# Seven half-size products for a down projection, with attention regrouped, in a PE-bound fused kernel

## The chip, the cores and the metric

The kernel runs on one core of a Trainium2 chip. The metric is device time in microseconds (us). TensorE (PE) does the matmuls, VectorE (DVE) and ScalarE (ACT) read its results out of PSUM, GpSimd (POOL) works in SBUF, and the queues of SP, ACT and POOL start transfers. A profile is one execution recorded by the hardware; its span is a little shorter than the timed runs of the same kernel (301.4 against 302.2 us before).

## The reference, cut to what matters

```python
k_p = k.reshape(B, H, Sp, 8, D).mean(axis=3)      # v_p likewise; B = H = 8, S = 576, Sp = 72, D = 64
attn = softmax(q @ k_p.T / sqrt(D));  x = attn @ v_p          # -> 4608 tokens x 512
h = x @ w_in                                       # 512 -> 2048, "up"
g = h * cos(h)
out = g @ w_out                                    # 2048 -> 512, "down"
```

## The kernel before: the parts that the change and the argument touch

Tokens go in nine tiles of 512. Tile t runs an up stage and a down stage; between the down matmuls of tiles 1 to 6 stands the attention of batch t+1, cut into four units (256 tokens x 4 heads), and of a rest segment (the last 64 tokens of batch t, all heads). PSUM has eight banks: three pairs, used in turn by the up stage and by attention, and two single banks for the down sums.

```python
def up_g(t, fp, between=()):                       # 8 per tile
    cos = ...; nc.scalar.activation(out=cos, in_=h, func=ACTF.Sin, bias=half_pi[:, :1])
    nc.vector.tensor_mul(out=g_sb[:, 2 * fp:2 * fp + 2, :], in0=h, in1=cos)

def down_mm(o, ms, fc):                            # 64 per tile, 512 columns each
    nc.tensor.matmul(o, lhsT=g_sb[:, fc, ms * 128:(ms + 1) * 128], rhs=w_out_sb[fc // 4][:, fc % 4, :], ...)

def values(b, u, pair, later=None):                # values and sums of one unit in one matmul, two halves
    ...
    for hp in range(2):
        nc.scalar.activation(out=lnc[half[1 - hp]], in_=pair[half[1 - hp], hp, 0:w], func=ACTF.Ln)
    nc.scalar.activation(out=inv, in_=lnc, func=ACTF.Exp, scale=-1.0)      # 1/sum
    ...                                            # two half multiplies into xT

def pool_add(b, which):                            # POOL sums of k and v for batch b
    add(out=s, in0=x[:, :, 0:4, :], in1=x[:, :, 4:8, :], op=ADD)           # one 4.06 us instruction
    ...
# steady tile: attention spread over the 64 down matmuls
fill = [(4, scores_of((b, us[0], 2), (b, us[1], 0))), (14, V_(0, 1, later)), (16, lambda: later.pop()()),
        (19, V_(1, 2)), (35, scores_of((b, us[2], 0), (b, us[3], 1), (t, REST, 2))),
        (38, V_(2, 0)), (43, lambda: values(t, REST, banks[1])), (46, V_(3, 2))]
```

The softmax here doesn't subtract the row's maximum and nothing guards it: scores larger than these inputs give would overflow.

## Time and profile before

| | before |
|---|---|
| time, median of the runs beside the changed kernel | 302.17 us |
| steady tile (tiles 2 to 6) | 31.30 us |
| up stage / rest of the tile | 13.85 / 17.45 us |
| PE's part of the chain that ended last | 93% |
| DVE, ACT, POOL busy | 57%, 68%, 43% |

The chain that ended last is followed back from the last instruction: each piece is what released the next one. Where it consists of PE pieces alone, nothing but PE's own stream sets the time. The prediction below shows those lines.

### The profile page before, as it was taken

The numbers are of one execution on the slowest core, as the hardware profiler recorded it, in microseconds if no ns is written. First come the engines' busy times: TensorE is split into PE (matmuls) and PEld (weight loads), VectorE is DVE, ScalarE is ACT, GpSimd is POOL, SyncE is SP. The second block draws the span as 40 slices with busy tenths as digits, with TensorE's granted clock in tenths as the row PEclk, the third lists the DMA queues.
The fourth block names the chain that finished last, engine by engine and source line by source line (L and its number), as shares of the span: only waits on it lengthen the run. The fifth ranks groups of instructions, "written<-read, shape, count | busy, mean of one in ns | idle before, by whom it ended". The sixth has DMA issues, their size and how long they took to land.

```text
span 301.4 us, 4625 instructions
## 1 busy us (share of the span) xinstructions
PE 293.9 (97%) x1816; PEld 143.2 (48%) x1816; DVE 170.8 (57%) x212; ACT 205.7 (68%) x254; POOL 130.4 (43%) x93
## 2 busy tenths in 40 slices
PE   8789999999999999999999999999999999999995
PEld 3445544445544454445444544455444544444444
DVE  5448637465467446754666556654775477425712
ACT  3786798469876987688778886789668966605500
POOL 8463016984983398239913990389300000000000
PEclk9999999999999999999999999999999999999999
DMA  7999999639526961697079617791811130131023
GB/s 152 197 207 206 206 205 195 141 55 176 117 60 124 167 127 29 146 158 140 6 170 143 129 36 171 94 174 39 141 32 35 37 70 0 37 70 35 0 67 75
DMA packets 44165, 32.91 MB, mean 109 GB/s; under 512 B 22128, under 2 KB 39408, under 8 KB 44144
## 3 DMA queue, kind: packets, MB, share of 16 engines
q0 software_dynamic: 19744, 18.07, 38.3%
q1 hardware_dynamic: 24160, 14.42, 20.5%
q8 instruction: 14, 0.23, 0.3%
q10 hardware_dynamic: 240, 0.13, 0.2%
q14 instruction: 7, 0.06, 0.1%
HBM read 36.70 MB, written 9.44 MB: 153 GB/s over the span
## 4 chain that ended last, share of the span: by engine, by line
PE 93%; DMA 4%; POOL 1%; DVE 1%; issue 0%; POOLq 0%; DVEq 0%
PE bank L297 41%; PE obank L310 41%; PE bank L241 5%; DMA kv_st<-in_v_dram 4%; PE bank L211 3%; PE bank L328 1%; PE bank L165 1%; POOL q_b L84 1%; PE obank L157 0%; PE obank L280 0%; PE obank L192 0%; DVE xT L282 0%; DVE vz L167 0%; POOL kv_st L84 0%; DVE o_sb L316 0%
## 5 line engine op out<-in xcount | busy, mean ns | idle before, releaser
L310 PE MATMUL obank<-w_out_sb,g_sb 128*128 128x512 bf16 x560 | 131.4, 379 | 0.0
L297 PE MATMUL bank<-xT,w_in_sb 128*128 128x512 bf16 x576 | 126.6, 379 | 0.0
L304 ACT ACTIVATE cos<-bank,half_pi 128x1024 f32<-128x1024 f32 x72 | 79.3, 1113 | 59.5 <-PE bank L297 59.5
L307 DVE TENSOR_TENSOR g_sb<-bank,cos 128x1024 bf16<-128x1024 f32 x72 | 87.3, 1223 | 43.0 <-ACT cos L304 42.9
L297 PEld LDWEIGHTS <-w_in_sb 128*128 128x128 bf16 x576 | 56.1, 98 | 67.6 <-issue 1.6
L310 PEld LDWEIGHTS <-g_sb 128*128 128x128 bf16 x560 | 52.8, 98 | 56.5 <-issue 2.0
L252 DVE TENSOR_TENSOR xT<-bank,inv 64x512 bf16<-64x512 f32 (+1 forms) x72 | 45.3, 629 | 40.8 <-ACT inv L248 40.1
L141 POOL TENSOR_TENSOR kv_st<-kv_st 72x2048 f32<-72x2048 bf16 x12 | 48.7, 4058 | 33.9 <-DMA kv_st<-in_k_dram 33.9
L247 ACT ACTIVATE lnc<-bank 64x512 f32<-64x512 f32 (+1 forms) x72 | 39.2, 544 | 3.1 <-PE bank L241 1.7
L316 DVE COPY o_sb<-obank 128x512 f32<-128x512 f32 x35 | 23.6, 689 | 30.9 <-PE obank L310 30.5
L218 ACT ACTIVATE ex<-bank 72x1024 bf16<-72x1024 f32 (+1 forms) x40 | 35.0, 929 | 8.5 <-PE bank L211 8.4
L142 POOL TENSOR_TENSOR kv_st<-kv_st 72x1024 f32<-72x1024 f32 x12 | 28.2, 2349 | 1.0
L248 ACT ACTIVATE inv<-lnc 128x512 f32<-128x512 f32 (+1 forms) x36 | 21.0, 583 | 1.1
L241 PE MATMUL bank<-ex,vz 72*128 72x256 bf16 (+1 forms) x176 | 20.0, 243 | 0.0
L241 PEld LDWEIGHTS <-vz 72*128 72x128 bf16 x176 | 13.6, 97 | 9.6 <-DVE xT L252 0.5
L145 POOL TENSOR_TENSOR kp<-kv_st 72x512 bf16<-72x512 f32 x12 | 14.9, 1263 | 0.5
L211 PE MATMUL bank<-qT,kk 64*72 64x256 bf16 (+1 forms) x192 | 13.2, 252 | 0.0
L211 PEld LDWEIGHTS <-kk 64*72 64x72 bf16 x192 | 7.4, 109 | 9.9 <-issue 7.2
L285 ACT ACT_TABLE_LOAD x9 | 11.5, 1283 | 0.9 <-PEq L519 0.7
L499 POOL COPY gate<-kk 1x1 bf16<-1x1 bf16 x5 | 0.9, 179 | 25.7 <-DMA kk<-kp 25.7
L288 ACT ACT_TABLE_LOAD x9 | 11.5, 1283 | 0.2
L103 POOL DMA_DIRECT2D kv_st<-in_v_dram x6 | 5.0, 841 | 8.8 <-PE bank L165 8.8
(55 smaller groups left out, 93.1 us busy)
## 6 DMA issues: line engine op xcount, KB each, us to landing
out_dram<-o_sb SPq DMA_DIRECT2D x70, 128.0 KB, 2.4
kv_st<-in_v_dram POOLq DMA_DIRECT2D x8, 576.0 KB, 13.7
kv_st<-in_k_dram POOLq DMA_DIRECT2D x7, 576.0 KB, 7.6
q_b<-in_q_dram POOLq DMA_DIRECT2D x6, 576.0 KB, 9.9
w_in_sb<-in_moe_w_in_dram POOLq DMA_DIRECT2D x4, 512.0 KB, 14.5
w_out_sb<-in_moe_w_out_dram POOLq DMA_DIRECT2D x4, 512.0 KB, 18.1
q_b<-in_q_dram POOLq DMA_DIRECT2D x4, 288.0 KB, 13.0
g_sb<-in_k_dram SPq DMA_DIRECT2D x1, 576.0 KB, 3.7
```

Source lines behind the costliest of these rows:

```text
L141: add(out=s, in0=x[:, :, 0:4, :], in1=x[:, :, 4:8, :], op=ADD)
L142: add(out=s[:, :, 0:2, :], in0=s[:, :, 0:2, :], in1=s[:, :, 2:4, :], op=ADD)
L211: nc.tensor.matmul(pair[:Sp, bank, c:c + n].rearrange("p (g n) -> p g n", n=64), lhsT=kk[b % 2][half[r], h0 + i, 0:Sp], rhs=att["qT", b][h ...
L218: nc.scalar.activation(out=ex[:, 0:nh * n].rearrange("p (a n) -> p a n", a=2), in_=pair[:Sp, :, 0:nh * n // 2], func=ACTF.Exp, scale=scale ...
L241: nc.tensor.matmul(pair[:, hp, (i // 2) * n:(i // 2 + 1) * n], lhsT=vz[b % 2][:, pj, 2 * hp:2 * hp + 2, :].rearrange("p a d -> p (a d)"), ...
L247: nc.scalar.activation(out=lnc[half[1 - hp]], in_=pair[half[1 - hp], hp, 0:w], func=ACTF.Ln)
L252: nc.vector.tensor_mul(out=x_out(b, u, half[hp]), in0=cols(pair[half[hp], hp, :], u), in1=cols(inv[half[1 - hp]], u))
L297: nc.tensor.matmul(h[:, j, :], lhsT=w_in_sb[fc // 4][:, ki, (fc % 4) * 128:(fc % 4 + 1) * 128], rhs=xT[:, ki, t * TILE:(t + 1) * TILE], st ...
L304: nc.scalar.activation(out=cos, in_=h, func=ACTF.Sin, bias=half_pi[:, :1])
L307: nc.vector.tensor_mul(out=g_sb[:, 2 * fp:2 * fp + 2, :], in0=h, in1=cos)
L310: nc.tensor.matmul(o, lhsT=g_sb[:, fc, ms * 128:(ms + 1) * 128], rhs=w_out_sb[fc // 4][:, fc % 4, :], start=(fc == 0), stop=(fc == FFCH - 1))
L316: nc.vector.tensor_copy(out=o[:, 0:n], in_=ps)
```

## The change

The intent is to do less on PE. A block product of 2 x 2 blocks takes seven half-size products of sums in place of eight. Three sums of the weights (w2, w3, w4) and one difference in place are made once; four sums of g (g1 to g4) are made on DVE in each tile; the products collect in the two down banks, and copies and adds take results out between them. Since DVE gets new work, attention is regrouped so that sums and values lie on all 128 partitions: half as many logarithms and multiplies. POOL's sums are cut into pieces of 512 elements. From tile 1 on the up stage takes the two halves of its 2048 columns in turns, so that g1 and g2 can be formed while it runs.

```diff
+    def values_of(parts, later):
+        weights = (lambda b, h: ones[:Sp, :]), (lambda b, h: vz[b % 2][:, h // 2, 3 * (h % 2), :])
+        for bank in range(2):                      # sums in one bank of the pair, values in the other
+            for b, u, pair in parts: ... nc.tensor.matmul(pair[hp * 64:hp * 64 + 64, bank, ...], ...)
+        for b, u, pair in parts: ... Ln, Exp; later.append(multiply)
 ...
+        A, Bb = obanks[1], obanks[0]
+        products = [
+            (A, True, part(g_part(0, 0, 0, HF)), of(w_out_sb[0:2])),
+            (A, False, part(g_part(1, 0, 0, HF)), of(w_out_sb[2:4])),
+            (Bb, True, part(g2), of(w2)),
+            (A, True, part(g1), of(w_out_sb[0:2], 1)),
+            (Bb, False, part(g3), of(w3)),
+            (A, False, part(g4), of(w_out_sb[2:4], 1)),
+            (Bb, False, part(g_part(1, 1, 0, HF)), of(w4)),
+        ]
+        reads = [
+            lambda: nc.scalar.copy(out=p1, in_=A),
+            lambda: nc.scalar.copy(out=o1[:, :, 0:HM], in_=two(A)),
+            lambda: add(v16, Bb, p1),
+            lambda: add(q15, A, p1),
+            lambda: add(o2[:, :, HM:], two(Bb), two(q15)),
+            lambda: (add(o1[:, :, HM:], two(A), two(v16)), rows_out(t, 0, o1)),
+            lambda: (add(o2[:, :, 0:HM], two(Bb), two(p1)), rows_out(t, 1, o2)),
+        ]
 ...
+            first = [(b, us[i], banks[i]) for i in range(3)] if steady else ...
+            second = [(b, us[3], banks[0]), (t, REST, banks[1])] if steady else []
+            product(0); reads[0](); exp_tables()          # (cut and joined)
+            scores of first;  product(1); reads[1](); g3
+            product(2); reads[2](); g4a;  product(3); reads[3](); g4b
+            values_of(first, later); later.pop(0)()
+            product(4); reads[4]();  the other multiplies
+            scores of second;  product(5); reads[5]()
+            values_of(second, later), multiplies;  product(6); reads[6]()
 ...
+                if n in range(41, 59, 3):                 # tile 0: the six weight sums on DVE
+                    weights.pop(0)()
```

Products are counted from 1 in the text: "product 1" is `product(0)`.

More of the change, by code (lines that the diff above doesn't have):

```diff
@@ L13 @@
 ADD = mybir.AluOpType.add
+SUB = mybir.AluOpType.subtract
 POOL = 8
@@ L64 @@
     g_sb = wpool.tile([128, FFCH, TILE], BF16, name="g_sb")
+    HF, HT, HM = FFCH // 2, TILE // 2, d_model // 2
+    g1, g2, g3, g4 = [wpool.tile([128, HF, HT], BF16, name=f"g{i}") for i in range(1, 5)]
+    w2, w3, w4 = [[wpool.tile([128, 4, HM], BF16, name=f"w{k}{i}") for i in range(2)] for k in range(2, 5)]
     SpA = -(-Sp // 16) * 16
@@ L70 @@
     vz = [wpool.tile([Sp, KCH, 4, D], BF16, name=f"vz{i}") for i in range(2)]
+    half_sums = wpool.tile([Sp, H, POOL // 2, D], FP32, name="half_sums")
     banks = [psum.tile([128, 2, 512], FP32, name=f"bank{i}") for i in range(3)]
@@ L86, in kv_tile @@
     def kv_tile():
-        return kvst.tile([128, 2 * H * POOL * D], BF16, name="kv_st", tag="kv_st")
+        return kvst.tile([128, 2 * KCH * ROW * D], BF16, name="kv_st", tag="kv_st")
     def even_part(st, i):
@@ L100, in load_kv @@
     def load_kv(b, which, src):
-        st = kv_tile()[:Sp].rearrange("p (i h t d) -> p i h t d", i=2, h=H, t=POOL)
-        nc.gpsimd.dma_start(out=st[:, 0].rearrange("p h t d -> p h (t d)"),
+        st = kv_tile()[:Sp, 0:H * POOL * D].rearrange("p (h t d) -> p h t d", h=H, t=POOL)
+        nc.gpsimd.dma_start(out=st.rearrange("p h t d -> p h (t d)"),
                             in_=src[b].rearrange("h (p t) d -> p h (t d)", t=POOL))
@@ L136, in pool_add @@
         st = staged.pop((which, b))
-        x = st[:, 0]
-        s = st[:, 1].rearrange("p h t d -> p (h t d)").bitcast(FP32).rearrange(
-            "p (h t d) -> p h t d", h=H, t=POOL // 2)
+        x, s = st, half_sums
         add = nc.gpsimd.tensor_tensor
-        add(out=s, in0=x[:, :, 0:4, :], in1=x[:, :, 4:8, :], op=ADD)
-        add(out=s[:, :, 0:2, :], in0=s[:, :, 0:2, :], in1=s[:, :, 2:4, :], op=ADD)
+        for h in range(0, H, 2):
+            add(out=s[:, h:h + 2], in0=x[:, h:h + 2, 0:4, :], in1=x[:, h:h + 2, 4:8, :], op=ADD)
+        for h in range(0, H, 4):
+            add(out=s[:, h:h + 4, 0:2, :], in0=s[:, h:h + 4, 0:2, :], in1=s[:, h:h + 4, 2:4, :], op=ADD)
         if which == "k":
@@ L230, in inverse_tile @@
     def inverse_tile(w):
-        lnc = asb.tile([128, 512], FP32, name="lnc", tag="lnc", bufs=1)
         inv = asb.tile([128, 512], FP32, name="inv", tag="inv", bufs=3)
-        return lnc[:, 0:w], inv[:, 0:w]
+        return inv[:, 0:w]
     def values(b, u, pair, later=None):
@@ L244, in values @@
         w = nh * n // 2
-        lnc, inv = inverse_tile(w)
+        inv = inverse_tile(w)
         for hp in range(2):
-            nc.scalar.activation(out=lnc[half[1 - hp]], in_=pair[half[1 - hp], hp, 0:w], func=ACTF.Ln)
-        nc.scalar.activation(out=inv, in_=lnc, func=ACTF.Exp, scale=-1.0)
+            nc.scalar.activation(out=inv[half[1 - hp]], in_=pair[half[1 - hp], hp, 0:w], func=ACTF.Ln)
+        nc.scalar.activation(out=inv, in_=inv, func=ACTF.Exp, scale=-1.0)
         def mul():
@@ L258, in values @@
             later.append(mul)
+    def values_of(parts, later):
+        weights = (lambda b, h: ones[:Sp, :]), (lambda b, h: vz[b % 2][:, h // 2, 3 * (h % 2), :])
+        for bank in range(2):
+            for b, u, pair in parts:
+                (c0, n), (h0, nh) = u
+                ex = att["ex", b, u]
+                for i in range(nh):
+                    hp = i % 2
+                    nc.tensor.matmul(pair[hp * 64:hp * 64 + 64, bank, (i // 2) * n:(i // 2 + 1) * n],
+                                     lhsT=weights[bank](b, h0 + i), rhs=ex[:, ex_col(u, i):ex_col(u, i) + n])
+        for b, u, pair in parts:
+            att.pop(("ex", b, u))
+            w = u[1][1] * u[0][1] // 2
+            inv = inverse_tile(w)
+            nc.scalar.activation(out=inv, in_=pair[:, 0, 0:w], func=ACTF.Ln)
+            nc.scalar.activation(out=inv, in_=inv, func=ACTF.Exp, scale=-1.0)
+            later.append(lambda b=b, u=u, pair=pair, inv=inv: nc.vector.tensor_mul(
+                out=x_out(b, u, slice(0, 128)), in0=cols(pair[:, 1, :], u), in1=cols(inv, u)))
     def sums_first(b, u, cs):
@@ L268, in sums_first @@
         w = nh * n // 2
-        lnc, inv = inverse_tile(w)
-        nc.scalar.activation(out=lnc, in_=cs[:, 0:w], func=ACTF.Ln)
-        nc.scalar.activation(out=inv, in_=lnc, func=ACTF.Exp, scale=-1.0)
+        inv = inverse_tile(w)
+        nc.scalar.activation(out=inv, in_=cs[:, 0:w], func=ACTF.Ln)
+        nc.scalar.activation(out=inv, in_=inv, func=ACTF.Exp, scale=-1.0)
         att["inv", b, u] = inv
@@ L288, in sin_tables, with up_order, up_bank @@
         nc.scalar.preload_act_table_set("trig_and_small")
+    def up_order(t):
+        n = FFCH // 2
+        return range(n) if t == 0 else [i + a * n // 2 for i in range(n // 2) for a in range(2)]
+    def up_bank(t, fp):
+        return banks[list(up_order(t)).index(fp) % 3]
     def up_mm(t, fp, k0=0, k1=KCH):
-        h = banks[fp % 3]
+        h = up_bank(t, fp)
         for j in range(2):
@@ L301, in up_g @@
     def up_g(t, fp, between=()):
-        h = banks[fp % 3]
+        h = up_bank(t, fp)
         cos = msb.tile([128, 2, TILE], FP32, name="cos", tag="cos", bufs=2)
@@ L311, in down_mm, with down_out @@
                          rhs=w_out_sb[fc // 4][:, fc % 4, :], start=(fc == 0), stop=(fc == FFCH - 1))
-    def down_out(t, ms, ps, c0=0, queues=(nc.sync, nc.sync)):
-        o = msb.tile([128, d_model], FP32, name="o_sb", tag="o_sb", bufs=6)
-        n = ps.shape[1]
-        nc.vector.tensor_copy(out=o[:, 0:n], in_=ps)
+    def down_out(t, ms, ps):
+        o = msb.tile([128, 2, d_model], FP32, name="o_two", tag="o_two", bufs=3)[:, 0]
+        nc.vector.tensor_copy(out=o, in_=ps)
         rows_of = out.rearrange("(b p t) m -> b t p m", b=B, t=ROW)
@@ L319, in down_out @@
             b_, pos = divmod((t * TILE + ms * 128) // 64 + i, ROW)
-            queues[i].dma_start(out=rows_of[b_, ORDER[pos], :, c0:c0 + n], in_=o[rows, 0:n])
-    def last_chunk():
-        t, ms = NT - 1, 3
-        for i, (c0, n) in enumerate(((0, 256), (256, 128), (384, 128))):
-            ps = banks[i][:, 0, 0:n]
-            for fc in range(FFCH):
-                nc.tensor.matmul(ps, lhsT=g_sb[:, fc, ms * 128:(ms + 1) * 128],
-                                 rhs=w_out_sb[fc // 4][:, fc % 4, c0:c0 + n],
-                                 start=(fc == 0), stop=(fc == FFCH - 1))
-            down_out(t, ms, ps, c0, (nc.sync, nc.scalar))
@@ L334, with put_weights @@
-    EX = 5
-    warm = consts.tile([128, 512], BF16, name="warm")
+            nc.sync.dma_start(out=rows_of[b_, ORDER[pos]], in_=o[rows])
+    def put_weights():
+        vec = nc.vector.tensor_tensor
+        parts = [[(w[:, :, 0:HM], w[:, :, HM:]) for w in (w_out_sb[i], w_out_sb[i + 2])] for i in range(2)]
+        for i, ((b11, b12), (b21, b22)) in enumerate(parts):
+            yield lambda i=i, x=b22, y=b12: vec(out=w3[i], in0=x, in1=y, op=SUB)
+            yield lambda i=i, y=b11: vec(out=w2[i], in0=w3[i], in1=y, op=ADD)
+            yield lambda i=i, x=b21: vec(out=w4[i], in0=x, in1=w2[i], op=SUB)
@@ new lines, in put_first_weights, with g_part, put_g12 @@
+    def put_first_weights(i):
+        w = w_out_sb[i]
+        nc.vector.tensor_tensor(out=w[:, :, HM:], in0=w[:, :, HM:], in1=w[:, :, 0:HM], op=SUB)
+    def g_part(f, t, f0, f1):
+        return g_sb[:, f * HF + f0:f * HF + f1, t * HT:(t + 1) * HT]
+    def put_g12(fp):
+        f0, f1 = 2 * fp, 2 * fp + 2
+        vec = nc.vector.tensor_tensor
+        vec(out=g1[:, f0:f1], in0=g_part(0, 1, f0, f1), in1=g_part(1, 1, f0, f1), op=ADD)
+        vec(out=g2[:, f0:f1], in0=g1[:, f0:f1], in1=g_part(0, 0, f0, f1), op=SUB)
@@ new lines, in put_g3, with put_g4, down_products, of @@
+    def put_g3(i):
+        f0, f1 = 4 * i, 4 * i + 4
+        nc.vector.tensor_tensor(out=g3[:, f0:f1], in0=g_part(0, 0, f0, f1), in1=g_part(0, 1, f0, f1), op=SUB)
+    def put_g4(i):
+        f0, f1 = 4 * i, 4 * i + 4
+        nc.vector.tensor_tensor(out=g4[:, f0:f1], in0=g_part(1, 0, f0, f1), in1=g2[:, f0:f1], op=SUB)
+    def down_products(t):
+        def of(w, m=0):
+            return lambda fc: w[fc // 4][:, fc % 4, m * HM:(m + 1) * HM]
+        def part(x):
+            return lambda fc, p: x[:, fc, p * 128:(p + 1) * 128]
+        A, Bb = obanks[1], obanks[0]
[8 more added lines that the diff above has]
+        ]
+        mms = []
+        for bank, first, g, w in products:
+            for fc in range(HF):
+                for p in range(2):
+                    mms.append(lambda bank=bank, first=first, g=g, w=w, fc=fc, p=p: nc.tensor.matmul(
+                        bank[:, p * HM:(p + 1) * HM], lhsT=g(fc, p), rhs=w(fc),
+                        start=(first and fc == 0 and p == 0), stop=(fc == HF - 1 and p == 1),
+                        skip_group_check=not first))
+        p1, v16, q15 = [msb.tile([128, d_model], FP32, name=n, tag=n, bufs=1) for n in ("p1_sb", "v_sb", "q_sb")]
+        o1, o2 = [msb.tile([128, 2, d_model], FP32, name="o_two", tag="o_two", bufs=3) for _ in range(2)]
+        two = lambda x: x.rearrange("p (a m) -> p a m", a=2)
+        add = lambda out, in0, in1: nc.vector.tensor_tensor(out=out, in0=in0, in1=in1, op=ADD)
+        reads = [
[7 more added lines that the diff above has]
+        ]
+        return [mms[i * 2 * HF:(i + 1) * 2 * HF] for i in range(7)], reads
@@ L336, with rows_out @@
+    def rows_out(t, tk, o):
+        rows_of = out.rearrange("(b p t) m -> b t p m", b=B, t=ROW)
+        for p in range(2):
+            for i, rows in enumerate(half):
+                b_, pos = divmod((t * TILE + tk * HT + p * 128) // 64 + i, ROW)
+                nc.sync.dma_start(out=rows_of[b_, ORDER[pos]], in_=o[rows, p])
+    EX = 4
+    warm = g4.rearrange("p f n -> p (f n)")[:, 0:512]
     nc.vector.memset(warm, 1.0)
@@ L357 @@
     make_identity(nc, identity)
-    dist = consts.tile([128, ROW, Sp], FP32, name="dist")
-    sign = consts.tile([128, ROW, Sp], FP32, name="sign")
-    groups = consts.tile([128, ROW, Sp], BF16, name="groups")
+    dist, sign = [x.rearrange("p f n -> p (f n)").bitcast(FP32)[:, 0:ROW * Sp].rearrange("p (t n) -> p t n", t=ROW)
+                  for x in (g1, g2)]
+    groups = g3.rearrange("p f n -> p (f n)")[:, 0:ROW * Sp].rearrange("p (t n) -> p t n", t=ROW)
     nc.vector.tensor_tensor(out=dist, in0=row_of.unsqueeze(2).to_broadcast([128, ROW, Sp]),
@@ L427 @@
         if t > 0:
-            up_mm(t, 0, 0, 2)
-            up_mm(t, 1, 0, 2)
-        for fp in range(FFCH // 2):
-            up_mm(t, fp, 2 if fp < 2 else 0)
+            for fp in up_order(t)[0:2]:
+                up_mm(t, fp, 0, 2)
+        for n, fp in enumerate(up_order(t)):
+            up_mm(t, fp, 2 if n < 2 else 0)
             between = ()
@@ L443 @@
             up_g(t, fp, between)
+            if t == 1 and n in (2, 4):
+                put_first_weights(n // 2 - 1)
+            if 0 < t and n % 2:
+                put_g12(n // 2)
             if 0 < t and b < B:
-                if fp == 0:
+                if n == 0:
                     q_transpose(b)
-                elif fp == 2:
+                elif n == 2:
                     k_transpose(b)
@@ L470 @@
                         (32, lambda: later.pop()()), (32, V_(2, 2)), (40, V_(3, 0))]
-        elif b < B:
-            us = BY_TOKENS
-            def scores_of(*parts):
-                def go():
-                    for f in scores_mm, scores_exp:
-                        for b_, u, bank in parts:
-                            f(b_, u, banks[bank])
-                return go
-            fill = [(4, scores_of((b, us[0], 2), (b, us[1], 0))), (14, V_(0, 1, later)), (16, lambda: later.pop()()),
-                    (19, V_(1, 2)), (35, scores_of((b, us[2], 0), (b, us[3], 1), (t, REST, 2))),
-                    (38, V_(2, 0)), (43, lambda: values(t, REST, banks[1])), (46, V_(3, 2))]
@@ L485, with product @@
-        fi = 0
-        if t == NT - 1:
-            mms = mms[:-FFCH]
-        for n, (ms, fc) in enumerate(mms):
-            while fi < len(fill) and fill[fi][0] <= n:
-                fill[fi][1]()
-                fi += 1
-            down_mm(obanks[ms % 2], ms, fc)
-            if fc == FFCH - 1:
-                down_out(t, ms, obanks[ms % 2])
+        if t == 0:
+            fi = 0
+            weights = list(put_weights())
+            for n, (ms, fc) in enumerate(mms):
+                while fi < len(fill) and fill[fi][0] <= n:
+                    fill[fi][1]()
+                    fi += 1
+                down_mm(obanks[ms % 2], ms, fc)
+                if fc == FFCH - 1:
+                    down_out(t, ms, obanks[ms % 2])
+                if n in range(41, 59, 3):
+                    weights.pop(0)()
+        else:
+            products, reads = down_products(t)
+            def product(i):
+                for mm in products[i]:
+                    mm()
+            us = BY_TOKENS
+            steady, rest = b < B, t < B
+            first = [(b, us[i], banks[i]) for i in range(3)] if steady else [(t, REST, banks[1])] if rest else []
+            second = [(b, us[3], banks[0]), (t, REST, banks[1])] if steady else []
+            later = []
+            product(0)
+            reads[0]()
+            if rest:
+                exp_tables()
+            for part in first:
+                scores_mm(*part)
+            for part in first[:1]:
+                scores_exp(*part)
+            product(1)
+            reads[1]()
+            for part in first[1:]:
+                scores_exp(*part)
+            for i in range(2):
+                put_g3(i)
+            product(2)
+            reads[2]()
+            put_g4(0)
+            product(3)
+            reads[3]()
+            put_g4(1)
+            if first:
+                values_of(first, later)
+                later.pop(0)()
+            product(4)
+            reads[4]()
+            for mul in later:
+                mul()
+            later = []
+            if second:
+                for part in second:
+                    scores_mm(*part)
+                for part in second:
+                    scores_exp(*part)
+            product(5)
+            reads[5]()
+            if second:
+                values_of(second, later)
+                for mul in later:
+                    mul()
+            product(6)
+            reads[6]()
@@ L505 @@
             pool_add(b + 1, "v")
-    last_chunk()
 _INS = ['q', 'k', 'v', 'moe_w_in', 'moe_w_out']
```

## The prediction

> **What bounds the kernel now.** I read the page of the kernel before first: which engine is busy, and of what the chain that ended last is made.
>
> ```profile
> PE 293.9 (97%) x1816; PEld 143.2 (48%) x1816; DVE 170.8 (57%) x212; ACT 205.7 (68%) x254; POOL 130.4 (43%) x93
> ...
> PE 93%; DMA 4%; POOL 1%; DVE 1%; issue 0%; POOLq 0%; DVEq 0%
> ```
>
> PE's busy share alone proves little, but 93% of the chain is PE too, so PE's stream of instructions is the time. The chain in order of time gives one steady tile (from one up projection, L297, to the next) and the tail:
>
> ```profile
> 16.52 0.43 PE obank L280 x4
> ...
> 17.78 0.63 PE obank L280 x8
> ...
> 116.75 13.85 PE bank L297 x64
> 130.59 0.86 PE obank L310 x4
> 131.46 0.56 PE bank L211 x8
> 132.02 2.26 PE obank L310 x10
> ...
> 139.70 0.86 PE bank L211 x16
> ...
> 144.16 3.89 PE obank L310 x18
> 148.05 13.85 PE bank L297 x64
> ...
> 256.00 0.26 PE bank L211 x8
> ...
> 284.04 10.36 PE obank L310 x48
> 294.40 3.55 PE bank L328 x48
> 297.97 0.29 DVE o_sb L316
> ```
>
> Columns: start, length, what. A tile takes 148.05 - 116.75 = 31.30 us: 13.85 up (64 matmuls of 512 columns, 216 ns each) and 17.45 for the rest (64 down matmuls, 13.85, scores and values between). No other engine appears: all waits are hidden. The timeline at the seam from up to down shows what they hide behind:
>
> ```profile
> 130.43 1.03 PE L310 MATMUL obank<-w_out_sb,g_sb 128*128 128x512 bf16 x4
> 130.63 1.11 ACT L304 ACTIVATE cos<-bank,half_pi 128x1024 f32<-128x1024 f32 x1 [0.61 <-PE bank L297]
> ...
> 131.76 1.28 ACT L285 ACT_TABLE_LOAD   x1
> 131.78 1.23 DVE L307 TENSOR_TENSOR g_sb<-bank,cos 128x1024 bf16<-128x1024 f32 x1 [0.50 <-ACT cos L304]
> ...
> 133.80 4.05 POOL L141 TENSOR_TENSOR kv_st<-kv_st 72x2048 f32<-72x2048 bf16 x1 [5.25 <-DMA kv_st<-in_k_dram]
> ```
>
> With T = 130.43, the end of the up stream: the last cosine ends at T+1.31, the table load at T+2.6, the last g product at T+2.6. The old down order needs that last g only at its 15th matmul, T+3.
>
> **What the Trainium skill says.** "TensorE: Matmul & The Clock Gate", section Back-to-back issue gap, gives 262 cycles for 256 columns, 109 ns. The trace agrees: L328 is 16 matmuls of 256 columns and 32 of 128, at 109 and 56 ns 3.5 us, and it took 3.55; so weight loads don't limit half-width matmuls. "TensorEngine Tiling (Array Packing)", section Key Properties, says that changing the tiling mode drains the engine. The 8 paired score matmuls took 0.56 us where 4 x 0.109 = 0.44 is the work, so 0.12 (in starts 0.2) for the change: I use 0.15 a block. "VectorE: DVE Perf Modes", section on the perf-mode tiers, has a bf16 tensor-tensor in SBUF at two elements a cycle, 1224 ns for 2048. My estimate from it: 0.42 us for 512 elements, 0.69 for 1024. Nothing in this trace shows such an operation. "SBUF — State Buffer", section Who interferes with whom: a DVE instruction with two SBUF inputs and a GpSimd one that reads SBUF exclude each other for a whole instruction. The kernel before has no such DVE work in its tiles, so its trace cannot confirm it; all new sums are of this kind.
>
> **The change, part by part.**
> *Down matmul, tiles 1 to 8.* 7 products x 16 = 112 matmuls of 256 columns: 112 x 0.1094 = 12.25 us for 13.85, so 1.60 us less PE work a tile, 12.8 in all. That is the intended gain.
>
> *Attention.* A unit's sums and values become separate matmuls on 64-column tiles, two at a time. The start of the kernel before does this already: 8 of L280 take 0.63 and 4 take 0.43, so four more cost 0.20, 50 ns each. PE work stays 2.0 us a tile, but there are four mode blocks for two: +0.3 us. ACT loses half of its logarithms (72 of 0.54 us on 64 partitions) and DVE half of its multiplies (72 of 0.63), neither of which bounds.
>
> *New sums on DVE.* Eight of 0.42 in the up stage, four of 0.69 later, 6.2 us a tile. Up stage, per two steps (3.46 us of PE): two g products of 1.22, two sums, some 0.1 us of waits for its own results: 3.4. It just fits.
>
> *The order of waits.* Product 2 adds onto the bank that ACT must have copied after product 1; attention must fill such gaps. The compiled order shows two table loads where there was one: before the copy, and again before the exponential. I follow a steady tile by hand from T, ends of matmuls showing 0.17 us later:
> 1. Product 1 runs T to T+1.85 (the last g but one arrives at about T+1.35, slightly late). Scores of unit 1 want no more; unit 2 writes the bank of the last g, free at T+2.65, then unit 3 to T+3.1. ACT: cosine to 1.31, first load to 2.6, copy (0.58) to 3.2, so product 2 starts at T+3.3. Without waits it would be 2.65: **wait 1, 0.65 us.**
> 2. Product 2 to T+5.05, product 3 to 6.8, product 4 to 8.55 (its bank was read by ACT at about 6.1: hidden). Values of group one to about T+10, product 5 to 11.75. Logarithm and exponential, 0.60 and 0.63, make the three inverses ready at about 10.3, 11.5, 12.8.
> 3. Second group: unit 4's scores need the first multiply (about T+11.5), fine. The rest segment's scores need bank 1, hence unit 2's multiply; but on DVE's in-order list the read of product 5 stands in front of that multiply. So PE waits 0.17 + 0.69 (read) + 0.69 (multiply) + 0.1 after product 5, less the 0.35 of unit 4's scores: **wait 2, 1.3 us.**
> 4. Product 6, values of group two, product 7 (1.75). The next up stage needs the rest segment in xT: after unit 4's sums, 0.17 + 0.60 + 0.63 + 0.38 + 0.42 on ACT with 0.15 of gaps, and 0.42 + 0.1 on DVE are 2.9 us; PE fills 2.3 (values 0.55, product 7). **Wait 3, 0.6 us.**
>
> Sum after up: 12.25 + scores 0.99 + values 1.98 + four blocks 0.6 + waits 2.55 = 18.4 for 17.45: **+0.9 us a tile**, six tiles (1 to 6): +5.5.
>
> *Tile 7* has only the rest segment. The wait for the copy (to T+3.3) is barely filled: 3.3 + 6 x 1.75 + values 0.5 = 14.3 for 14.2 (256.00 to 270.20): +0.1. *Tile 8* has no attention: product 2 waits to T+2.7, product 7 ends at 2.7 + 6 x 1.75 = T+13.2, read to T+14.1, and then four writes of 128 KB go out behind a whole tile's second half, where the kernel before had only 64 rows of 128 columns in each last write. Before: 301.4 - 284.04 = 17.4. After, with about 4 us for the writes (they land in 2.4 when single; an estimate): 18.2. **+0.8.**
>
> *Once only.* Six weight sums of 0.69 in tile 0's down stage and two in tile 1's up stage stand on DVE while POOL is at its first sums (busy from 47.8 to 64.6 in the trace before). With exclusion in turns, each can wait for a POOL piece of about 1.1 us (the 4.06 us sum in four). DVE then comes late to tile 1's first g products, and there is little spare to catch up. Without exclusion I get 1.3 us of PE wait, in full turns 7: **+4.**
>
> Sum: +5.5 + 0.1 + 0.8 + 4 = +10.4 on 302.3: about 312.5; I say 312.
>
> **Rivals.**
> *The products pay and the waits hide*: 302.3 - 12.8 + 6 x 0.3 for modes = 291. For it speaks the spare of ACT and DVE (68% and 57%) and that half their attention work goes. Against it: waits 1 to 3 are set by order, not by load, and each follows from durations in the trace.
> *Only part of the waits appears* (say wait 1 and 3 halved, POOL exclusion mild): -1.6 + 0.3 + 1.9 a tile, +3.6, with tile 7, 8 and the once-only part +2: about 308. Possible.
> *DVE becomes the bound of the up stage*: if the sums run at one element a cycle (0.69 for 512), two steps take 2.45 + 1.38 + 0.1 = 3.9 for 3.46, +1.9 us a tile, and with POOL's sums reaching further into up stages more: 325. The operands are packed bf16, which speaks against.
> *Transfers*: bytes are unchanged, and no steady DMA is in the chain; nothing.
>
> **Range and chances.** Waits 1 to 3 are sums of known durations, good to 0.3 us each, so about 4 us over six tiles; the once-only part is uncertain by 3 either way. I predict 312 us, with 304 to 319 as the range. Slower by over 2% means over 308.4: 0.74. Within 2%: 0.22. Faster than 296.3: 0.04.
>
> **What would show it.** In the profile after: PE's share of the chain falls from 93%, with DVE and ACT pieces of waits 1 to 3 in each tile; a tile of 32.2 us, of which up is 13.85; in the seam a copy between two table loads; PE's score block of the rest segment waiting for the xT multiply; DVE sums of 0.42 and 0.69 us, longer beside POOL work; the largest single loss at tile 1. I would be wrong if the tile takes under 31 us (waits hidden by something I put in the wrong order), if up stages stretch beyond 14.5 us in steady tiles (DVE bound), or if mode changes around the 64-column matmuls cost well over 0.2 us.

## The result, and the profile after

The changed kernel took 319.88 us (median; 319.25 to 320.25), the kernel before 302.17 on the same chip. The ratio is 1.058 (95% interval 1.057 to 1.060): slower by 5.8%. A ratio here is the mean time of one kernel's fast runs over that of the other's of the same rounds, so it is not quite the ratio of the medians. The direction was right; the time lies just above the stated range (304 to 319), and the loss of 17.7 us is nearly twice the 9.8 predicted.

From the page of the changed kernel: busy time by engine, granted PE clock in 40 slices, and who makes up the chain.

```profile
PE 289.1 (91%) x2320; PEld 180.7 (57%) x2320; DVE 217.7 (68%) x291; ACT 203.7 (64%) x246; POOL 147.4 (46%) x141
...
PEclk9999999869999999999999999999999999999997
...
PE 73%; DVE 14%; ACT 8%; issue 3%; ACTq 0%; DVEq 0%
```

PE's part of the chain fell from 93% to 73%, and 22% of it are DVE and ACT pieces now, though neither engine is busier than 68%. This is not PE's idle time: PE, busy for 91% of the span, works beside some of these pieces. The dip to 8 and 6 in the clock row is new too; it lies at tile 1. The chain in order of time (start, length, what) for one steady tile, from up stage to up stage:

```profile
125.80 14.02 PE bank L333 x64
139.84 1.12 ACT cos L340
140.99 1.24 DVE g_sb L343
142.26 0.63 PE bank L221 x8
142.90 5.40 PE obank L409 x48
148.30 1.43 PE bank L278 x24
149.73 1.87 PE obank L409 x16
151.62 0.69 DVE o_two L417
152.32 0.61 DVE xT L286
152.97 0.33 PE bank L221 x8
153.29 1.85 PE obank L409 x16
155.14 0.70 PE bank L278 x16
155.87 0.61 ACT inv L284
...
157.88 0.43 DVE xT L286
158.35 14.02 PE bank L333 x64
```

The tile takes 158.35 - 125.80 = 32.55 us. Wherever an ACT or DVE piece stands in this list, PE stood still for part of it, and the three places are the three waits of the prediction: the last cosine and g product before unit 2's scores (139.84 to 142.26), the read of product 5 and the multiply before the rest segment's scores (151.62 to 152.97), and the logarithms, exponentials and multiplies before the next up stage (155.87 to 158.35, partly covered by product 7).

Where the 16.6 us of span went, from the starts of the up stages in PE's records of the two profiles (rounded):

| stretch | before | after | difference |
|---|---|---|---|
| up to tile 1's first matmul | 53.99 | 53.24 | -0.8 |
| tile 1 | 31.3 | 40.0 | +8.7 |
| tiles 2 to 6 | 156.5 | 162.8 | +6.3 |
| tile 7 | 28.3 | 28.1 | -0.2 |
| tile 8 to the end | 31.4 | 33.9 | +2.5 |

Tile 1 is where the prediction was furthest off. The timeline there (start, length, engine, line, what, and in brackets the idle time before it with its cause):

```profile
52.87 1.64 DVE L363 TENSOR_TENSOR w<-w,w_out_sb 128x1024 bf16<-128x1024 bf16 x1
...
56.10 1.75 DVE L362 TENSOR_TENSOR w<-w_out_sb,w_out_sb 128x1024 bf16<-128x1024 bf16 x1
...
57.38 5.70 POOL L150 TENSOR_TENSOR half_sums<-kv_st 72x512 f32<-72x512 bf16 x4
...
62.21 2.35 DVE L343 TENSOR_TENSOR g_sb<-bank,cos 128x1024 bf16<-128x1024 f32 x2
...
63.48 11.20 PE L333 MATMUL bank<-xT,w_in_sb 128*128 128x512 bf16 x40 [4.89 <-DVE g_sb L343]
```

The weight sums took 1.27 to 1.75 us each instead of 0.69, and POOL's four pieces 5.70 us where undisturbed ones took 4.48. DVE came to the first g product at 62.2, the up stage ran out of banks, and PE idled for 4.89 us. Then PE's clock fell. By stretches of 4 us (busy time of each engine, then the granted clock, DMA share and GB/s):

```profile
60.00:64.00 4.00, 0.53 (x2) 0.25 (x2) 3.97 (x5) 0.48 (x1) 4.00 (x4) 0.69 0.28 61
64.00:68.00 4.00, 4.00 (x11) 1.32 (x10) 3.93 (x4) 1.55 (x2) 2.85 (x3) 0.50 0.98 195
```

Eleven matmuls in 4 us at a clock of 0.50, against eighteen or so at full clock. That looks like a large loss, but from 51.6 to 78 us DVE works without a gap and the chain runs through DVE; the account of the prediction below shows that the clock added little.

### The profile page after: what moved, and what is told of

Same layout as the page of the kernel before. It is cut to its first block, busy times and chain, and to the rows that moved or that the text cites. A ratio compares the mean times of both kernels' runs of the same rounds, so it can differ in the third digit from the quotient of the medians.

```text
span 318.0 us, 5705 instructions
## 1 busy us (share of the span) xinstructions
PE 289.1 (91%) x2320; PEld 180.7 (57%) x2320; DVE 217.7 (68%) x291; ACT 203.7 (64%) x246; POOL 147.4 (46%) x141
## 4 chain that ended last, share of the span: by engine, by line
PE 73%; DVE 14%; ACT 8%; issue 3%; ACTq 0%; DVEq 0%
PE bank L333 35%; PE obank L409 24%; DVE g_sb L343 5%; PE bank L278 4%; PE obank L346 3%; PE bank L221 2%; ACT cos L340 2%; ACT inv L285 2%; DVE xT L286 2%; ACT inv L284 2%; DVE o_two L417 2%; PE obank L494 1%; DVE w L363 1%; DVE w L362 1%; ACT ex L228 1%
## 5 line engine op out<-in xcount | busy, mean ns | idle before, releaser
L150 POOL TENSOR_TENSOR half_sums<-kv_st 72x512 f32<-72x512 bf16 x48 | 59.8, 1271 | 34.1 <-DMA kv_st<-in_k_dram 33.7
L409 PEld LDWEIGHTS <-g 128*128 128x128 bf16 x512 | 49.0, 98 | 7.1 <-issue 1.2
L152 POOL TENSOR_TENSOR half_sums<-half_sums 72x512 f32<-72x512 f32 x24 | 33.0, 1396 | 0.0
L284 ACT ACTIVATE inv<-bank 128x512 f32<-128x512 f32 (+1 forms) x31 | 16.7, 538 | 23.9 <-PE bank L278 23.9
L409 PE MATMUL obank<-w_out_sb,g_sb 128*128 128x256 bf16 x256 | 30.7, 272 | 1.0 <-ACT p_sb L419 1.0
L409 PE MATMUL obank<-w,g 128*128 128x256 bf16 x256 | 30.6, 273 | 0.0
L409 PE MATMUL obank<-w_out_sb,g 128*128 128x256 bf16 x256 | 30.6, 273 | 0.0
L286 DVE TENSOR_TENSOR xT<-bank,inv 128x512 bf16<-128x512 f32 (+1 forms) x31 | 19.5, 629 | 11.8 <-ACT inv L285 11.6
L285 ACT ACTIVATE inv<-inv 128x512 f32<-128x512 f32 (+1 forms) x31 | 18.0, 582 | 1.0
L346 PE MATMUL obank<-w_out_sb,g_sb 128*128 128x512 bf16 x64 | 15.7, 380 | 0.0
## 6 DMA issues: line engine op xcount, KB each, us to landing
kv_st<-in_v_dram POOLq DMA_DIRECT2D x8, 576.0 KB, 12.7
```

The lines of the kernel that those rows point to most:

```text
L150: add(out=s[:, h:h + 2], in0=x[:, h:h + 2, 0:4, :], in1=x[:, h:h + 2, 4:8, :], op=ADD)
L152: add(out=s[:, h:h + 4, 0:2, :], in0=s[:, h:h + 4, 0:2, :], in1=s[:, h:h + 4, 2:4, :], op=ADD)
L284: nc.scalar.activation(out=inv, in_=pair[:, 0, 0:w], func=ACTF.Ln)
L285: nc.scalar.activation(out=inv, in_=inv, func=ACTF.Exp, scale=-1.0)
L286: later.append(lambda b=b, u=u, pair=pair, inv=inv: nc.vector.tensor_mul(out=x_out(b, u, slice(0, 128)), in0=cols(pair[:, 1, :], u), in1=c ...
L409: mms.append(lambda bank=bank, first=first, g=g, w=w, fc=fc, p=p: nc.tensor.matmul(bank[:, p * HM:(p + 1) * HM], lhsT=g(fc, p), rhs=w(fc), ...
```

## The experiments

Eleven kernels ran on the same chip. The medians of the kernel before beside them were 301.98 to 302.16 us. Times are medians. The changed kernel itself was not run again, so it is compared through its ratio to the kernel before.

### Weight sums earlier

```diff
-                if n in range(41, 59, 3):
+                if n in (17, 19, 22, 26, 28, 30):
```

> The six weight sums of tile 0 are put earlier (down matmul 17 to 30 instead of 41 to 56), before POOL starts its sums at about 46.6 us. Theory (weight sums and POOL sums exclude each other in turns, DVE comes late to tile 1, PE idles 4.9 us and its clock falls to half): the weight sums take 0.69 us each instead of 1.27 to 1.75, PE idles under 0.5 us at tile 1 and stays at full clock, the time falls by 5 to 6.5 us to about 314. Rival (the eight weight sums are simply too much DVE work beside tile 1's g products): the sums still have to be done, the time falls by under 2 us.

It took 318.67 us (ratio to before 1.055, interval 1.051 to 1.059): about 1.2 us less than the changed kernel by the medians, and no difference that the intervals can tell (1.058 lies inside). The total is what the rival forecast, but not for its reason. At tile 1 the theory held: PE's up stage ran without a wait, the clock stayed at 1.00, and the tile took 33.3 us (59.34 to 92.68) instead of 40.0. The loss had moved into tile 0:

```profile
46.05 1.58 DVE L363 TENSOR_TENSOR w<-w,w_out_sb 128x1024 bf16<-128x1024 bf16 x1
...
49.84 1.86 PE L346 MATMUL obank<-w_out_sb,g_sb 128*128 128x512 bf16 x4 [2.63 <-DVE o_two L351]
```

DVE runs in order, and multiplies in front of the weight sums were late, so the last two still met POOL's sums (from 45.9 us on), and behind them stood the copies that free the down banks. PE idled 2.63 us and its clock was 0.50 from 52 to 56 us. The place was badly chosen, so the total does not test the exclusion. The lengths agree with it: four weight sums ahead of POOL's took 0.68 to 0.69 us, the two beside it 1.58 and 1.52.

### Fills in place of the weight sums

```diff
-            yield lambda i=i, x=b22, y=b12: vec(out=w3[i], in0=x, in1=y, op=SUB)
-            ...
+            for w in (w3, w2, w4):
+                yield lambda w=w[i]: nc.vector.memset(w, 0.01)
```

> Wrong results on purpose: the six weight sums of tile 0 are replaced by six fills of the same tiles at the same places on DVE, 1024 elements each, which read nothing. Theory (the loss at tile 1 is the exclusion of DVE sums and POOL sums, not DVE's amount of work): though a fill is longer than a sum alone (about 0.9 to 1.1 us against 0.69), the fills are not stretched, PE does not idle over 1.5 us at tile 1, its clock stays full, and the time falls by 4 to 6.5 us to 313.5 to 316. Rival (DVE's amount of work at that place): no fall, 319 or more.

It took 316.01 us, 3.9 less than the changed kernel, at the upper end of what was expected. The fills, beside the same POOL work, were not stretched:

```profile
56.87 0.91 DVE L363 MEMSET w<- 128x1024 bf16 x1 [0.16 <-issue]
...
60.28 10.48 PE L333 MATMUL bank<-xT,w_in_sb 128*128 128x512 bf16 x40 [2.02 <-DVE g_sb L343]
```

Each fill took 0.91 us, longer than a sum alone, and yet DVE was back 3.2 us earlier. So what stretches the sums is that they read SBUF beside POOL, not the amount of DVE work. But PE still idled 2.02 us, more than the 1.5 expected, and its clock still fell to 0.69 in one stretch of 4 us. The fills are not free: with the gaps between them they kept DVE for 6.3 us (51.50 to 57.78), where six undisturbed sums need 4.1. So the 3.9 us are less than what the exclusion costs.

### Tile 1 as before

```diff
-            if t == 1 and n in (2, 4):
+            if t == 1 and n > 4:
+                weights.pop(0)()
+            if t == 2 and n in (2, 4):
                 put_first_weights(n // 2 - 1)
-            if 0 < t and n % 2:
+            if 1 < t and n % 2:
                 put_g12(n // 2)
 ...  tile 1: old up order, old down matmuls and attention; three more weight sums at its down matmuls 2, 6, 10
```

> Tile 1 uses the down matmul, the attention and the up order of the kernel before; the products start at tile 2; the six weight sums go to the end of tile 1's up stage and the start of its down stage, where POOL waits for data. Theory (weight sums in turns with POOL's sums at the start of tile 1 cost 6.5 us with the fallen clock): these are gone, and tile 1 takes 31.3 instead of 32.55 and more: about 312, clock 1.0 throughout, weight sums 0.69 us each. Rival (the sums cost wherever they stand, as the failed early placement suggests): over 316.

It took 311.11 us (ratio 1.030): 8.8 less, a little more than expected. All weight sums took 0.68 to 0.69 us, since POOL was waiting for data then, and the clock stayed at 0.998. Tile 1 took 31.29 us (52.70 to 83.99). The edit changes several things at once (tile 1 also drops the products and the new attention, worth 1.25 us), so the rest, 7.5 us, is the once-only part as a whole; its pieces are read from the traces below.

### POOL's sums whole

```diff
-        for h in range(0, H, 2):
-            add(out=s[:, h:h + 2], in0=x[:, h:h + 2, 0:4, :], in1=x[:, h:h + 2, 4:8, :], op=ADD)
+        add(out=s, in0=x[:, :, 0:4, :], in1=x[:, :, 4:8, :], op=ADD)
 ...  (and the second sum likewise)
```

> POOL's sums are done whole again (one 4.06 us and one 2.35 us instruction) with everything else as changed. Theory (a DVE sum with two SBUF inputs waits for the whole POOL instruction and the reverse): DVE sums of 0.42 and 0.69 us beside POOL work become up to 4.7 us long, tile 1 starts at least as late as now and g sums of steady tiles reach into the waits of PE: slower than the changed kernel by 1 to 8 us, 321 to 328. Rival (each instruction only slows the other by sharing a port, no whole-instruction lock): lengths of DVE sums hardly change, time within 1 us of 320.

It took 335.14 us (ratio 1.110), 15 us slower than the changed kernel, more than the 1 to 8 expected. One weight sum of the timeline:

```profile
55.91 4.38 POOL L149 TENSOR_TENSOR half_sums<-kv_st 72x2048 f32<-72x2048 bf16 x1
56.30 4.54 DVE L360 TENSOR_TENSOR w<-w_out_sb,w_out_sb 128x1024 bf16<-128x1024 bf16 x1
```

The POOL instruction ended at 60.29 us and the sum 0.55 us later, at 60.84: nearly all of its 4.54 us was waiting. A wait that lasts as long as the other engine's instruction is a lock, not a shared rate. PE idled 9.81 us at tile 1 (4.89 in the changed kernel), and over the run its scores waited 12.7 us for multiplies into xT (6.2 there). Cutting the sums was thus a necessary part of the change.

### Multiplies before the read

```diff
-            reads[4]()
             for mul in later:
                 mul()
             later = []
+            reads[4]()
```

> On DVE the multiplies of units 2 and 3 stand before the read of product 5 instead of behind it. Theory (wait 2, 1.2 us a tile, is the rest segment's scores waiting for a multiply that stands behind that read): the wait falls to 0.7 us, set by the second inverse on ACT, so 0.5 us in each of six tiles, 3 us in all: 317. Rival (something else sets the wait, for example the inverse alone): no change, 320.

It took 317.09 us (ratio 1.050), 2.8 less. In its chain the steady tile takes 157.15 - 125.03 = 32.12 us, 0.43 less than the changed kernel's; the piece before the rest segment's scores is no longer the read but the second inverse on ACT and its multiply. So wait 2 was set by DVE's order, and behind it stands ACT.

### One table load

```diff
             product(0)
-            reads[0]()
             if rest:
                 exp_tables()
+            reads[0]()
```

> The changed kernel with the request for the exponential's table placed before the copy, which leaves one table load per down stage instead of two. Theory (the copy waits for the first load in either case, and the exponentials have about 1.8 us to spare before the values): no change, 319 to 320.5. Rival (ACT's 1.28 us more in each of seven tiles is on the path): 7 to 9 us less.

It took 319.18 us (ratio 1.057, interval 1.054 to 1.059, against 1.058): no change that the runs can tell, as expected. Seven table loads of 1.28 us were removed from an engine and nothing came of it, because that stretch of ACT was not on the path.

### Attention alone

The kernel before, with only its `fill` of tiles 1 to 6 exchanged (the helper `values_of` of the change and two small functions that call it are left out here):

```diff
+            fill = [(9, scores_of((b, us[0], 0), (b, us[1], 1), (b, us[2], 2))), (36, values_go(first)),
+                    (37, muls_go), (46, scores_of((b, us[3], 0), (t, REST, 1))), (55, values_go(second)),
+                    (56, muls_go)]
```

> The kernel before (64 down matmuls, no new sums) with only the attention of tiles 1 to 6 in two groups, sums and values apart, at the same places of the down stage. Theory (waits 1 and 3 and the mode changes belong to the grouping, not to the products): 0.3 us for modes, 0.3 for the wait on the last g's bank and 0.4 for the last multiplies a tile, 1.0 us in six tiles: 308. Rival A (only the products bring the waits): 302 to 304. Rival B (the 64-column matmuls themselves are slow): the values blocks take clearly over 1.4 us in the trace.

It took 313.59 us (ratio 1.038): 11.6 us slower than before, twice the expected loss. A steady tile takes 152.43 - 119.25 = 33.18 us, 1.88 more than before. Its chain shows the same three places, and among them, again,

```profile
145.90 0.70 DVE xT L277
...
146.64 0.33 PE bank L211 x8
```

the rest segment's scores waiting for unit 2's multiply, which I had thought gone without the reads. So the grouping alone, at these places, loses more than the whole change does in a steady tile (1.25), and the products win part of it back. Rival B falls: the values block of 24 matmuls kept PE for 1.4 us, as the paired 64-column matmuls should.

### Products alone

The seven products as changed, one table load, and the attention of the kernel before, unit by unit, laid over the 112 product matmuls (the list in words):

```diff
+            fill = [(11, scores_mm of units 1, 2), (16, scores_exp of units 1, 2), (27, values unit 1, multiply later),
+                    (30, that multiply), (36, values unit 2), (61, scores of units 3, 4 and the rest segment),
+                    (66, values unit 3), (75, values rest), (80, values unit 4)]
```

> The seven products and their sums as changed, but the attention of tiles 1 to 7 unit by unit with sums and values in one matmul and the old bank order, spread over the products at about the old times, and a single table load per down stage. Theory (products save 1.60 us of PE work a tile and only wait for the copy after product 1, about 0.85; the grouping brings waits 2 and 3): a steady tile of 30.2 us, and with tile 7 and the once-only and tail losses of the changed kernel (6.5 and 2.5) about 304. Rival (DVE, with halves of multiplies again, 26 us of work a tile and POOL in turns, cannot keep up): a steady tile over 31.5, time over 312.

It took 336.3 us (ratio 1.113). One steady tile took 34.45 us (130.62 to 165.07), the next two 35.87 and 35.14; the up stages were as fast as ever (13.86). The forecast failed, and the rival's numbers came true. DVE had the 26 us of work that the rival names (26.6), but that does not fill 34.45 us; its order was bad once more:

```profile
152.71 2.47 DVE L381 TENSOR_TENSOR g<-g_sb 128x1024 bf16<-128x1024 bf16 x2
...
155.20 1.39 DVE L261 TENSOR_TENSOR xT<-bank,inv 64x512 bf16<-64x512 f32 x2
...
156.64 0.33 PE L221 MATMUL bank<-qT,kk 64*72 64x64 bf16 x8 [2.57 <-DVE xT L261]
```

Unit 2's multiplies stood behind two g sums that took 2.47 instead of 1.29 us beside POOL, and the rest segment's scores waited for unit 2's bank. POOL's turns are only a part: the last steady tile, with hardly any POOL sums (3.24 us), still took 33.27. This run says that the old places of attention don't suit the products; it does not say what products alone could reach.

### The writes of the last tile

```diff
+    def cols_out(t, tk, o, m): ... (nc.sync, nc.scalar)[i].dma_start(... half of the columns ...)
+        if t == NT - 1:
+            reads[4] = lambda: (add_of[4](), cols_out(t, 1, o2, 1))
+            ...
```

> Only the writes of the last tile change: each half of the columns goes out when its sum is ready, in 64 KB writes on two queues. Theory (the last four 128 KB writes issued one after another on one queue take 6.1 us after the last sum, against 3.1 after the last copy of the kernel before): 2 to 2.5 us less, about 317.5. Rival (the end is the latency of a write whatever its size): under 0.7 us less.

It took 317.71 us (ratio 1.052), 2.2 less, as expected. In the changed kernel the last sum ends at 311.20 + 0.69 = 311.89 and the span at 318.0, 6.1 us later:

```profile
310.21 4.94 SPq L434 DMA_DIRECT2D out_dram<-o_two  x8
311.20 0.69 DVE L417 TENSOR_TENSOR o_two<-obank,p_sb 128x512 f32<-128x512 f32 x1 [1.05 <-PE obank L409]
```

One queue was still issuing until 315.15; a single write of 128 KB lands 2.4 us after its issue. With the writes split, 4.5 us remain after the last sum (311.69 to 316.2). But the number of queues is not shown to matter. Both kernels write 1.05 MB here, and the DMA engines (last two columns: busy share, GB/s) move it equally fast, the first line from the changed kernel, the second from this run:

```profile
311.40:316.40 5.00, 0.00 (x0) 0.00 (x0) 0.50 (x1) 0.00 (x0) 0.00 (x0) 0.77 0.93 205
309.40:314.40 5.00, 1.56 (x15) 1.15 (x12) 1.24 (x2) 0.00 (x0) 0.00 (x0) 1.00 0.88 203
```

The first write is issued at 308.23 instead of 310.21, as soon as half of the columns is ready: 2.0 us earlier, which is nearly all of the gain.

### Rearranged

Everything learnt so far in one kernel: tile 1 as before; product 2 in the other bank, so that nothing waits for the copy after product 1; units 1, 2 and the rest segment in the first group; split writes.

```diff
-            (A, False, part(g_part(1, 0, 0, HF)), of(w_out_sb[2:4])),
-            (Bb, True, part(g2), of(w2)),
+            (Bb, True, part(g_part(1, 0, 0, HF)), of(w_out_sb[2:4])),
+            (A, True, part(g2), of(w2)),
 ...
-            lambda: nc.scalar.copy(out=o1[:, :, 0:HM], in_=two(A)),
+            lambda: add(o1[:, :, 0:HM], two(Bb), two(p1)),
 ...
+            early = [(b, us[0], banks[0]), (b, us[1], banks[2])] if steady else []
+            late = [(t, REST, banks[1])] if rest else []
+            second = [(b, us[2], banks[0]), (b, us[3], banks[2])] if steady else []
```

> All of it: products from tile 2, product 2 in the other bank so that nothing waits for the copy after product 1 (the first output is then an add on DVE), units 1 and 2 and the rest segment in the first group, units 3 and 4 in the second, scores and values moved so that each multiply has a product to hide behind, one table load, the writes of the tail split. Theory (waits 1 to 3 are a matter of order): a steady tile of 29.9 us for 31.30, no wait over 0.3 us in it, about 293, 3% faster than the kernel before. Rival (with the order mended DVE or ACT is the bound, as DVE has about 23 us of work plus turns with POOL): a steady tile of 31 or more and no gain.

It took 299.53 us, ratio 0.991 (0.989 to 0.993): 20 us faster than the changed kernel and faster than the kernel before, but not the 293 forecast. Tile 1 as before and the split writes had given 8.8 and 2.2 us when made alone; some 9 us are left for the order. The seam wait is gone, as the chain of its tile 6 shows:

```profile
209.12 13.85 PE bank L333 x64
222.97 1.75 PE obank L409 x16
224.71 0.56 PE bank L221 x8
225.27 1.85 PE obank L409 x16
```

That tile, the only steady one without POOL sums beside it, takes 239.56 - 209.12 = 30.44 us; three others take 30.72, 30.82 and 31.58. There the two halves of a g sum stand on DVE beside POOL:

```profile
167.84 2.24 DVE L385 TENSOR_TENSOR g<-g_sb,g 128x1024 bf16<-128x1024 bf16 x2
```

2.24 us for what takes 1.36 alone, and the multiplies behind them are late. So the waits were mostly a matter of order. Of what is left over the 29.9 forecast, 0.5 us stays in the tile without POOL sums; DVE and POOL taking turns is the likely rest, up to 1.1 us in the others.

### Rearranged once more

```diff
-            put_g4(1)                              # was before values_of(first)
+            put_g4(1)                              # now behind the three multiplies
             some(4, 0, 6)
-            scores_all(second)
-            some(4, 6, 16)
+            scores_all(second[:1])
+            some(4, 6, 12)
+            scores_all(second[1:])
+            some(4, 12, 16)
```

(and the two in-place weight sums at the very start of tile 2)

> The rearranged kernel once more: the second half of the fourth sum goes behind the multiplies on DVE, unit 4's scores six matmuls later, the two in-place weight sums before tile 2's up stage where DVE is idle. Theory (what is left over the ideal 29.9 us a tile is DVE sums taking turns with POOL, which delays the multiplies that scores wait for): steady tiles of 30.2 to 30.7 instead of 30.7 to 31.6, 2 to 3 us less, about 297. Rival (the inverse on ACT sets the wait anyway): 299.

It took 298.58 us, ratio 0.988 (0.985 to 0.990), so about 1 us less and not 2 to 3; the two intervals just touch, so the gain itself is at the edge of what the runs can tell. Tiles 3 and 5 now take 30.44 us (tile 3: 116.17 to 146.61), but tiles 4 and 6 still 31.2 and 31.1, where g sums of the up stage meet the end of POOL's sums. This version beats both kernels: 1.2% faster than the one before, clear of the noise.

## Why the prediction was right or wrong

**Right: the mechanism.** The products do save 1.6 us of PE work a tile, new sums take 0.42 and 0.68 us where POOL is quiet (0.42 and 0.69 predicted), the up stage just fits (13.84 us from its start to the first product), transfers play no part before the last tile, and the three waits are the ones named, each in its place. Measured in the steady tile shown: wait 1, from the end of product 1 at 141.39 to the start of product 2 at 142.90, less 0.85 of scores and mode changes, is 0.66 (0.65 predicted); wait 2, from unit 4's scores done at about 151.74 to 152.97, is 1.2 (1.3); wait 3, from product 7 done at 157.63 to 158.35, is 0.7 (0.6). One detail of wait 1 differs: the prediction has the copy end last, by about 0.1 us, while in the trace the copy ends at 142.85 and the scores that waited for the last g product at 142.90. Two waits end within 0.05 us, so by this trace removing the copy alone would gain next to nothing; attention alone, which has no such copy, shows the wait for the last g product too.

**Mis-sized: "four blocks 0.6".** The steady tile lost 1.25 us, not 0.9. After the up stage it takes 158.35 - 139.64 = 18.7 us, of which products, scores and values are 15.2 and the waits 2.6. The rest, 0.9, is put down to the four mode blocks, 0.22 each (a difference, not measured block by block): the starts in the timeline before had shown 0.2, and I took 0.15. Over six tiles that is 2 us.

**Mis-sized: "Once only ... +4".** Tile 1 lost 8.7 us, of which 1.25 any tile loses: 7.4 for the once-only part. My figure for exclusion in full turns was 7, and I averaged it with the 1.3 of no exclusion. The step that failed is this averaging: full turns is what came. The six weight sums took 9.3 us on DVE where 4.1 is the work, and DVE reached tile 1's first g product 9.0 us after the tile's start (53.24 to 62.21), against 3.9 in the run with earlier weight sums: 5.0 us. The two g sums that followed took 2.6 us beside POOL instead of 0.85: 1.75 us more. Together these are 6.8 of the 7.4 us; the run with earlier sums, free of both, still loses 0.8 in tile 1 over a steady tile. The clock after the 4.9 us of idling was not in the prediction at all, but it cost little: from its first to its last g product of tile 1 DVE needed 14.9 us (62.21 to 77.08), and without the 1.75 that is the 13.1 us (63.28 to 76.41) of the run with earlier sums, whose clock stayed at 1.00.

**Mis-sized: "about 4 us for the writes".** The end came 6.1 us after the last sum: not four writes but all eight of the last tile, 1.05 MB, stand there, the first issued only 1.7 us before the last sum was done, and the DMA engines move them at about 205 GB/s. Tile 8 lost 2.5 us, not 0.8.

The three terms together, 2 + 3.4 + 1.7 = 7.1 us, less 0.8 for the earlier start and 0.3 at tile 7, are the 6 us between the 16.6 of the two profiled spans and the 10.4 of the prediction's own sum (the medians differ by 17.7). All three went the same way. The range allowed for the waits and the once-only part; for the mode blocks and the writes it allowed nothing.

**Two reasons of mine that fell on the way.** That the grouping costs 1.0 us a tile by itself was too low: it costs 1.9, as wait 2 does not need the reads. And that the old places of attention would suit the products was wrong by 4 us a tile.

What stays open: the expectation of 30.2 us for products alone was not tested well, since its order was bad. So how much of the saved PE work a well-placed old attention would leave is not known.

## What to carry to other kernels

When a kernel is bound by one engine with all else hidden, taking work off that engine exposes the order of the others: follow each bank and each in-order queue through a tile by hand before counting on the saving. Sums of two SBUF operands on DVE are not free beside POOL work, however idle DVE looks; put them where POOL waits for data, and cut POOL's instructions short. Here the seven products went from 5.8% slower to 1.2% faster by changing where and in which order things are done (tile 1 left as it was and the last writes split among them). The 3.6 us won are about a third of the 11.2 that the PE work saved in seven tiles promised.

## What the Trainium skill lacked or had wrong

- "SBUF — State Buffer", Who interferes with whom: the rule (a DVE instruction with two SBUF inputs and a GpSimd one that reads SBUF exclude each other) is borne out, 4.54 us for a 0.69 us sum beside a POOL instruction of 4.38. It lacks what a row of such instructions does: they take turns, so six sums of 0.69 took 1.27 to 1.75 us each beside POOL pieces of 1.1 to 1.3, and four POOL pieces 5.70 us instead of 4.48.
- "TensorEngine Tiling (Array Packing)", Key Properties: it says that changing the tiling mode drains the engine, but gives no cost. Here a block of scores or 64-column matmuls between full ones cost about 0.22 us, by difference.
- "TensorE: Matmul & The Clock Gate", Back-to-back issue gap: its sustained figures for weight load and matmul pairs (about 81 ns at 128 columns, about 131 at 512) are not met; 128 columns took 56 ns and 512 took 216, as its formula for the isolated gap says.
- "TensorE: Matmul & The Clock Gate", Why this matters for your kernels: it warns of idle gaps over about 3 us. Here an idle time of 4.89 us was followed by a clock of 0.50, and so was one of 2.63 us with 1.15 us shortly before (weight sums earlier). Even 2.02 us was followed by 0.69 over 4 us (fills), while 2.57 and 2.90 us left it at 1.00 (products alone). So a gap under 3 us is not safe, and its length alone does not decide.
